# Gated mix of an S4D convolution and a bilinear GLU: one column's split tokens made twice instead of stored, and the last two rows summed from PSUM

## Chip, cores and metric

One core of one Trainium2 chip. The metric is the device time of one execution in microseconds (us), the median of three runs. Every operand and result is in f32. The engines are named as in the profile: PE (TensorE), DVE (VectorE), ACT (ScalarE), POOL (GpSimd), and SP, whose queue issues most of the DMA transfers.

## What is computed

```python
def _A_ref(u, ...):                       # S4D: a long convolution per channel
    dt = jnp.exp(log_dt)
    A = -jnp.exp(log_A_real) + 1j * A_imag
    C = (C_real + 1j * C_imag) * dt[:, None]
    P = jnp.exp((A * dt[:, None])[:, :, None] * pos[None, None, :])
    K = 2.0 * jnp.einsum("dn,dnl->dl", C, P).real
    Kf = jnp.fft.rfft(K, L2)              # L2 = 4096
    Uf = jnp.fft.rfft(u_t, L2)
    y = jnp.fft.irfft(Uf * Kf[None, :, :], L2)[:, :, :L]
    return y + u * D_skip
def _B_ref(x, w_gate, w_up, w_down):      # bilinear GLU
    h = (x @ w_gate) * (x @ w_up)
    return h @ w_down
x = A_u
g = sigmoid((x * gate_w).sum(-1, keepdims=True))
return g * _A_ref(x, ...) + (1 - g) * _B_ref(B_x, ...)
```

L = 2048 tokens, D = 512 channels, N = 128 states, F = 1792 hidden columns of the GLU.

## The kernel before, in words

**Who sets the order.** The kernel's functions don't issue instructions; they hand them to a planner (`Work.add`), each with an engine, an assumed duration, the tiles that it reads and writes, and a rank. `Work.run` then takes, over and over, the instruction that can start earliest by these assumed durations; among equals the lower rank goes first, then the one handed in first. `InOrder` issues them at one line, so all of them stand at L119 in the profile, and groups are told apart by the names of their tiles. A tile belongs to a tag with a fixed number of buffers, and tiles of a tag get their buffers strictly in the order in which they were created. A change in a few calls can therefore move instructions far away from it.

**The GLU.** The tokens are cut into four columns of 512 (`ci`), the hidden columns into 14 pieces of 128 (`f`), the pieces into four groups: f 0 to 2, 3 to 5, 6 to 9, 10 to 13 (L24). The loop of `glu` runs over groups and, in each, over the columns: 0, 1, 2, 3 in the first and third group (`gi` 0 and 2), 3, 2, 1, 0 in the second and fourth. A group so begins with the column that the one before it ended with, and its tokens are not loaded again there. Column 0 is used at the start, at the end of the second group and the start of the third, and as the last of all.

Products are made of three fp32r matmuls (low × high, high × low, high × high), so each operand is held split in a high and a low half. `tokens(gi, ci, kt)` brings one of the four tiles of a column (128 channels by 512 tokens). In the first group it loads 256 KB from `xT` into a buffer of the tag `raw`, ACT casts the high half into `xs`, DVE subtracts for the low half, and the split tile of 512 KB is stored in DRAM (`xs_d`). In later groups it loads these 512 KB back. The tag `xs` has 5 buffers, `raw` has 2; `raw` also carries the loads of the weights (`load`, L405; `split`, L411; `high`, L427; `rest`, L431).

`hidden(f)` makes the two products pg and pu for a piece and a column (24 matmuls of 512 columns: 2 products × 4 token tiles × 3), ACT copies pg to h, DVE multiplies h by pu, ACT casts hh and DVE subtracts hl. `down` multiplies these with the down weights (`dhi`, `dlo`) for four rows of 128 tokens, in PSUM tiles `y` (2 buffers). `evacuate` (L581) takes a finished y: ACT scales it by 1 − g into `acc`, and the row is stored to `out` (first group, by SP) or added to it by a DMA (later groups, by POOL). In the last group's last column the rows are kept instead, and `ends` (L599) loads what `out` holds so far into a tile `kt`, DVE adds the last parts of the convolution and then acc, and SP stores the row.

**The convolution** runs between the GLU's products on the same engines, in 16 blocks. DVE and ACT make tables `x` and `v` (one buffer for v), PE multiplies them (`k<-v,x`), and transforms of the kernel (`k<-kt,w1k_t`) and of u (`k<-in,w2s`) follow, a product on DVE, inverse transforms, and round trips through DRAM (`sk_d`, `su_d`, `y_d`).

Of the kernel before, what the change touches and what calls it, by code (L numbers as in the profile page):

```python
# [14 lines left out]
ALU = mybir.AluOpType  # L15
# [3 lines left out]
P = 128  # L19
L, D, N, F = 2048, 512, 128, 1792  # L20
KT = D // P
# [4 lines left out]
LAST = 3 if len(GROUPS) % 2 else 0  # L26
# [138 lines left out]
class Work:  # L165
# [27 lines left out]
    def add(self, engine, us, fn, r=(), w=(), rank=1, after=0.0, dma=0, hold=(), rows=(), many=0):  # L193


        task = Task(len(self.tasks), engine, us, fn, rank, after, dma)
        task.rows, task.many = rows, many
        self.tasks.append(task)
        clash = lambda p, q: p is None or q is None or p == q
        split = lambda x: x if isinstance(x, tuple) else (x, None)  # L200
        for tile, part in map(split, r):
            task.deps.update(t for p, t in tile.writers if clash(p, part))
        for tile, part in map(split, w):
            task.deps.update(t for p, t in tile.writers + tile.readers if clash(p, part))
        for tile, part in map(split, r):
            tile.readers.append((part, task))
        for tile, part in map(split, w):
            tile.writers.append((part, task))
        for tile, _ in map(split, [*r, *w, *hold]):
            if tile.pool and tile not in task.tiles:  # L210
                task.tiles.append(tile)
                tile.users.append(task)
        task.deps.discard(task)
        return task
# [105 lines left out]
def gated_mix_kernel(  # L320
# [16 lines left out]
    pe, dve, act, sp, pool_q = (InOrder(tc, e) for e in (nc.tensor, nc.vector, nc.scalar, nc.sync, nc.gpsimd))  # L337
    uv = u.rearrange("(p r) d -> p r d", r=NR)
    ov = out.rearrange("(p r) d -> p r d", r=NR)
    work = Work()  # L340
    add = work.add
# [12 lines left out]
    m_su, m_sk, m_y, m_out, m_xs, m_turn = (work.memory() for _ in range(6))  # L354
# [5 lines left out]
    def new(pool, tag, shape, dtype=F32, bufs=1, loose=False):  # L360
        return work.tile(pools[pool], tag, shape, dtype, bufs, loose)
# [14 lines left out]
    ngate = const.tile([P, NR], F32, name="ngate")  # L376
    m_gate = work.memory()
# [27 lines left out]
    def load(key, src, rank=0):  # L405
        if key in raws:
            return
        t = raws[key] = new("glu", "raw", [P, D], bufs=2)
        add("sp", 0.42, lambda: sp.dma_start(t.t, src), w=[t], dma=256, rank=rank)

    def split(hi, lo, s, key):  # L411

        t = raws[key]
        t, k = t if isinstance(t, tuple) else (t, None)
        src = lambda: t.t if k is None else t.t[:, k]
        got = t if k is None else (t, k)
        s, z = s if isinstance(s, tuple) else (s, s)
        ph, pl = (hi, s), (lo, z)
        at = lambda x, s: x.t if s is None else x.t[:, s] if hi is lo else x.t[:, s * D : (s + 1) * D]
        add("act", 0.62, lambda: act.copy(at(hi, s), src()), r=[got], w=[ph], rank=0)  # L420
        add(
            "dve", 0.69,
            lambda: dve.tensor_tensor(out=at(lo, z), in0=src(), in1=at(hi, s).bitcast(F32), op=ALU.subtract),
            r=[got, ph], w=[pl], rank=0,
        )
# [49 lines left out]
    def weights(fs):  # L475
        for f in fs:
            ws[f] = [new("glu", n, [P, 2 * D], F32R, SLOTS) for n in ("whi", "wlo")]
            if f == 0:
                for kt in range(KT):
                    first_split(kt)  # L480
                    if kt + 1 < KT:
                        tokens(0, 0, kt + 1)
                continue
            for c in range(2):
                load(("w", f, c), wts[f][:, c * D : (c + 1) * D])
                if f in GROUPS[0]:
                    split(*ws[f], c, ("w", f, c))
                else:
                    high(ws[f][0], c, ("w", f, c))
            if f not in GROUPS[0]:  # L490
                rest(*ws[f], wts[f][:, : 2 * D], 2)
# [23 lines left out]
    def tokens(gi, ci, kt):  # L515

        x = xs[kt] = new("glu", "xs", [P, 2, D], F32R, 5)
        if gi:
            add("sp", 0.42, lambda: sp.dma_start(x.t.bitcast(F32), xs_d[ci, kt]), r=[(m_xs, (ci, kt))], w=[x], dma=512, rank=0)
            return  # L520
        load(("x", gi, ci, kt), xT[kt * P : (kt + 1) * P, ci * D : (ci + 1) * D])
        split(x, x, (0, 1), ("x", gi, ci, kt))
        add("sp", 0.42, lambda: sp.dma_start(xs_d[ci, kt], x.t.bitcast(F32)), r=[x], w=[(m_xs, (ci, kt))], dma=512, rank=2)

    THREE = ((1, 0), (0, 1), (0, 0))
# [53 lines left out]
    ending = []  # L579

    def evacuate(gi, ci, r, y):  # L581
        t = 4 * ci + r
        final = gi == len(GROUPS) - 1 and ci == LAST
        acc = new("glu", "raw", [P, D], bufs=2) if final and r == 3 else new("glu", "acc", [P, D], bufs=3)
        add(
            "act", 0.69, lambda: act.activation(acc.t, y.t, AF.Copy, scale=ngate[:, t : t + 1]),
            r=[y, (m_gate, ci)], w=[acc], rank=0,
        )
        if final:
            ending.append((r, acc))  # L590
        elif gi == 0:
            add("sp", 0.42, lambda: sp.dma_start(ov[:, t, :], acc.t), r=[acc], w=[(m_out, t)], dma=256)
        else:
            add(
                "pool", 0.95, lambda: pool_q.dma_start(ov[:, t, :], acc.t, accum_op=ALU.add),
                r=[acc, (m_out, t)], dma=640, rows=[t],
            )

    def ends():  # L599

        t0 = 4 * LAST
        sums = new("tab", "kt", [P, 4, D])
        add(
            "sp", 0.42, lambda: sp.dma_start(sums.t, ov[:, t0 : t0 + 4, :]),
            r=[(m_y, (KT - 1, 0))], w=[sums, *((m_out, t0 + r) for r in range(4))], dma=1024, rows=range(t0, t0 + 4),
        )
        for r, acc in ending:
            t = t0 + r
            for q, (fin, parts) in late["fin"].items():
                add(  # L610
                    "dve", 0.25,
                    lambda r=r, q=q, t=t, fin=fin: dve.scalar_tensor_tensor(
                        sums.t[:, r, P * q : P * q + P], fin.t[:, 4 * (LAST % 2) + r], gate[:, t : t + 1],
                        sums.t[:, r, P * q : P * q + P], op0=ALU.mult, op1=ALU.add,
                    ),
                    r=[*parts, (m_gate, LAST)], w=[(sums, (r, q))], rank=0,
                )
            add(
                "dve", 0.69,
                lambda r=r, acc=acc: dve.tensor_tensor(  # L620
                    out=sums.t[:, r], in0=acc.t, in1=sums.t[:, r], op=ALU.add
                ),
                r=[acc], w=[(sums, (r, q)) for q in range(KT - 2, KT)], rank=0,
            )
            add(
                "sp", 0.42, lambda r=r, t=t: sp.dma_start(ov[:, t, :], sums.t[:, r]), r=[(sums, (r, q)) for q in range(KT - 2, KT)], w=[(m_out, t)],
                dma=256, rank=-1,
            )

    def glu():  # L630
        order = [(gi, ci) for gi in range(len(GROUPS)) for ci in (range(4) if gi % 2 == 0 else range(3, -1, -1))]
# [4 lines left out]
        for n, (gi, ci) in enumerate(order):  # L636
            fs = GROUPS[gi]
            if ci != old:
                for kt in range(KT):
                    tokens(gi, ci, kt)  # L640
            old = ci
            hs = {f: hidden(f) for f in fs}
            ends = n % 4 == 3 and gi + 1 < len(GROUPS)
            if ends:
                weights(GROUPS[gi + 1])

            for rr in ((0, 1), (2, 3)):
                ys = {r: new("ps_y", "y", [P, D], bufs=2) for r in rr}
                late = fs[-1:] if rr[0] == 0 else []
                for r in rr:  # L650
                    for f in fs:
                        if f not in late:
                            down(ys[r], r, hs[f], wd[f], f == fs[0], f == fs[-1])
                    if not late:
                        evacuate(gi, ci, r, ys[r])
                if late:
                    for r in rr:
                        down(ys[r], r, hs[fs[-1]], wd[fs[-1]], False, True)
                        evacuate(gi, ci, r, ys[r])
            if ends:  # L660
                down_weights(GROUPS[gi + 1])
# [701 lines left out]
    for b in range(NB):  # L1363
# [10 lines left out]
        if b % 4 == 3:  # L1374
            transforms(b // 4)
    ends()

    work.run()
# [53 lines left out]
```

## Time and profile before

| | us |
|---|---|
| runs | 601.52, 602.17, 602.39 |
| median | 602.17 |
| profiled execution, own time | 601.78 |
| its span in the trace | 600.0 |

| engine | busy us | share of the span |
|---|---|---|
| PE | 585.8 | 98% |
| DVE | 512.3 | 85% |
| ACT | 401.0 | 67% |
| POOL | 128.9 | 21% |

The times are those of whole executions; the trace begins a little later and ends a little earlier, so its span is 1.8 us shorter than the execution that it shows. Stretches are counted from the span's start. A wait is an engine's idle time ahead of an instruction, with the instruction that ended it; a landing is the time from a DMA's issue until its bytes are there.

### The profile page before, as it was taken

The page shows a single profiled execution, that of the slowest core. Times are in us where ns is not written, and L with a number is a line of the kernel's source. Part 1 is how long each engine was busy: PE and PEld are TensorE (multiplying, and loading weights), DVE is VectorE, ACT ScalarE, POOL GpSimd, SP SyncE. Part 2 cuts the span into 40 slices and gives each one's busy share as a digit, 9 for nine tenths or more (in the row PEclk, how much of TensorE's full clock was granted, in tenths as well). Part 3 has the DMA queues.
Part 4 walks back from the last instruction along what each step waited for, and adds up shares of the span by engine and source line. Part 5 has one row for each costly group of instructions (what it writes and reads, how often), then busy time and mean ns, then how long its engine had stood idle before and what let it go on. Part 6 is the DMA issues. An engine that isn't in the chain of part 4 may idle for free.

```text
span 600.0 us, 15878 instructions
## 1 busy us (share of the span) xinstructions
PE 585.8 (98%) x6500; PEld 443.4 (74%) x6500; DVE 512.3 (85%) x811; ACT 401.0 (67%) x893; POOL 128.9 (21%) x191
## 2 busy tenths in 40 slices
PE   8899999999999999999999999999999999999996
PEld 5657777777877787887777877866878777767674
DVE  6999999999998997999999999978999933486525
ACT  5279787999678479967959764979984423433522
POOL 0011212221204131310133301104353023201111
PEclk9989999999999999999999999999999999999998
DMA  8899979699869699996959945999999569959976
GB/s 276 314 357 340 336 281 338 187 207 253 232 175 227 166 241 248 195 229 163 302 135 266 215 129 171 226 250 239 182 203 260 95 159 355 244 153 264 279 141 122
DMA packets 71867, 137.33 MB, mean 229 GB/s; under 512 B 7156, under 2 KB 35828, under 8 KB 69364
## 3 DMA queue, kind: packets, MB, share of 16 engines
q1 hardware_dynamic: 47476, 88.21, 45.9%
q0 software_dynamic: 23904, 47.98, 40.4%
q8 instruction: 51, 0.84, 0.6%
q10 hardware_dynamic: 416, 0.13, 0.1%
q14 instruction: 20, 0.16, 0.1%
HBM read 81.25 MB, written 55.05 MB: 227 GB/s over the span
## 4 chain that ended last, share of the span: by engine, by line
PE 79%; DVE 8%; ACT 6%; DMA 5%; issue 1%; ACTq 0%; DVEq 0%
PE y L119 22%; PE pu L119 21%; PE pg L119 21%; PE k L119 15%; DMA raw<-in_wts 4%; DVE x L119 2%; DVE y L119 1%; DVE v L119 1%; ACT ts L119 1%; ACT whi L119 1%; DMA y<-in_xT 1%; ACT L119 1%; DVE h L119 1%; DVE t L119 1%; DVE xs L119 1%
## 5 line engine op out<-in xcount | busy, mean ns | idle before, releaser
L119 PE MATMUL pg<-xs,whi 128*128 128x512 f32 x448 | 139.2, 392 | 1.0 <-DVE xs L119 0.7
L119 PE MATMUL pu<-xs,whi 128*128 128x512 f32 x448 | 138.7, 391 | 0.0
L119 PEld LDWEIGHTS pg<-xs,whi 128*128 128x128 f32 x448 | 84.5, 189 | 20.0 <-ACT whi L119 2.0
L119 PEld LDWEIGHTS pu<-xs,whi 128*128 128x128 f32 x448 | 84.4, 188 | 17.1
L119 PE MATMUL y<-dhi,hl 128*128 128x512 f32 x224 | 90.5, 404 | 2.2 <-DVE x L119 1.1
L119 PE MATMUL pu<-xs,wlo 128*128 128x512 f32 x224 | 90.1, 402 | 0.9 <-issue 0.5
L119 PE MATMUL pg<-xs,wlo 128*128 128x512 f32 x224 | 90.1, 402 | 0.8 <-ACT whi L119 0.5
L119 PE MATMUL y<-dlo,hh 128*128 128x512 f32 x224 | 87.5, 391 | 1.3 <-DVE dlo L119 1.3
L119 PE MATMUL y<-dhi,hh 128*128 128x512 f32 x224 | 87.4, 390 | 0.0
L119 POOL DMA_DIRECT2D out<-acc x44 | 38.4, 954 | 184.8 <-ACT acc L119 173.8
L119 ACT COPY ev<-k 128x512 f32<-128x512 f32 x112 | 59.2, 595 | 15.7 <-PE k L119 15.6
L119 ACT CAST hh<-h 128x512 fp32r<-128x512 f32 x56 | 34.7, 620 | 43.3 <-DVE h L119 43.2
L119 ACT ACTIVATE acc<-y,ngate 128x512 f32<-128x512 f32 x63 | 42.8, 686 | 30.6 <-PE y L119 28.2
L119 DVE TENSOR_TENSOR h<-pu,h 128x512 f32<-128x512 f32 x56 | 38.6, 689 | 23.0 <-PE pu L119 22.2
L119 PEld LDWEIGHTS y<-dhi,hl 128*128 128x128 f32 x224 | 42.0, 188 | 21.7 <-issue 6.2
L119 PEld LDWEIGHTS pu<-xs,wlo 128*128 128x128 f32 x224 | 42.1, 188 | 19.2 <-issue 9.8
L119 PEld LDWEIGHTS pg<-xs,wlo 128*128 128x128 f32 x224 | 42.0, 188 | 19.1 <-issue 6.8
L119 ACT COPY h<-pg 128x512 f32<-128x512 f32 x56 | 33.1, 590 | 29.7 <-PE pg L119 27.8
L119 PEld LDWEIGHTS y<-dlo,hh 128*128 128x128 f32 x224 | 42.1, 188 | 9.5 <-DVE dlo L119 1.7
L119 PEld LDWEIGHTS y<-dhi,hh 128*128 128x128 f32 x224 | 42.1, 188 | 9.1
L119 DVE TENSOR_TENSOR hl<-h,hh 128x512 fp32r<-128x512 f32 x56 | 38.5, 687 | 8.4 <-ACT hh L119 8.4
L119 POOL DMA_DIRECT2D su_d<-ev x32 | 17.3, 549 | 90.2 <-ACT ev L119 90.2
(127 smaller groups left out, 1015.7 us busy)
## 6 DMA issues: line engine op xcount, KB each, us to landing
xs<-xs_d SPq DMA_DIRECT2D x36, 512.0 KB, 7.8
out<-acc POOLq DMA_DIRECT2D x44, 256.0 KB, 7.1
raw<-in_wts SPq DMA_DIRECT2D x36, 256.0 KB, 5.2
xs_d<-xs SPq DMA_DIRECT2D x16, 512.0 KB, 7.1
su_d<-ev POOLq DMA_DIRECT2D x32, 256.0 KB, 5.3
y_d<-ts SPq DMA_DIRECT2D x14, 512.0 KB, 6.5
in<-su_d POOLq DMA_DIRECT2D x24, 256.0 KB, 8.4
sk_d<-ev SPq DMA_DIRECT2D x6, 1024.0 KB, 6.2
```

What stands on the lines that cost most here:

```text
L119: got = getattr(self.engine, name)(*args, **kw)
```

## The change

**Tokens.** In the first group the tiles of column 0 are split but no longer stored. At the end of the second group, where column 0 comes again, its tiles are loaded from `xT` and split again, and stored then; the fourth group reads them back as before.

**End.** In the last column of the last group, rows 2 and 3 aren't copied by ACT any more. DVE sums them with a multiply-add that reads y from PSUM and scales it by 1 − g. The last row is summed and stored in two halves of 256 columns, the second half by ACT's queue. Rows 0 and 1 are still copied, and DVE adds them with the same kind of instruction and scale 1.

```diff
     def tokens(gi, ci, kt):
...
-        if gi:
+        if gi > (ci == 0):
             add("sp", 0.42, lambda: sp.dma_start(x.t.bitcast(F32), xs_d[ci, kt]), r=[(m_xs, (ci, kt))], w=[x], dma=512, rank=0)
             return
         load(("x", gi, ci, kt), xT[kt * P : (kt + 1) * P, ci * D : (ci + 1) * D])
         split(x, x, (0, 1), ("x", gi, ci, kt))
+        if gi == 0 == ci:
+            return
         add("sp", 0.42, lambda: sp.dma_start(xs_d[ci, kt], x.t.bitcast(F32)), r=[x], w=[(m_xs, (ci, kt))], dma=512, rank=2)
...
     def evacuate(gi, ci, r, y):
...
-        acc = new("glu", "raw", [P, D], bufs=2) if final and r == 3 else new("glu", "acc", [P, D], bufs=3)
+        if final and r > 1:
+            ending.append((r, y))
+            return
+        acc = new("glu", "acc", [P, D], bufs=3)
...
-                    r=[*parts, (m_gate, LAST)], w=[(sums, (r, q))], rank=0,
+                    r=[*parts, (m_gate, LAST)], w=[(sums, (r, 1))], rank=0,
                 )
-            add(
-                "dve", 0.69,
-                lambda r=r, acc=acc: dve.tensor_tensor(
-                    out=sums.t[:, r], in0=acc.t, in1=sums.t[:, r], op=ALU.add
-                ),
-                r=[acc], w=[(sums, (r, q)) for q in range(KT - 2, KT)], rank=0,
-            )
-            add(
-                "sp", 0.42, lambda r=r, t=t: sp.dma_start(ov[:, t, :], sums.t[:, r]), r=[(sums, (r, q)) for q in range(KT - 2, KT)], w=[(m_out, t)],
-                dma=256, rank=-1,
-            )
+            for n, cs in enumerate((slice(0, D // 2), slice(D // 2, D)) if r == 3 else (slice(0, D),)):
+                part = [(sums, (r, k)) for k in (range(2) if r < 3 else (n,))]
+
+                def total(r=r, t=t, acc=acc, cs=cs):
+                    scale = 1.0 if r < 2 else ngate[:, t : t + 1]
+                    dve.scalar_tensor_tensor(
+                        sums.t[:, r, cs], acc.t[:, cs], scale, sums.t[:, r, cs], op0=ALU.mult, op1=ALU.add
+                    )
+
+                add("dve", 0.42 if r == 3 else 0.69, total, r=[acc, (m_gate, LAST)], w=part, rank=0)
+                e, q = ("act", act) if n else ("sp", sp)
+                add(
+                    e, 0.42, lambda r=r, t=t, cs=cs, q=q: q.dma_start(ov[:, t, cs], sums.t[:, r, cs]), r=part,
+                    dma=128 if r == 3 else 256, rank=-1,
+                )
```

The planner's order changes in many places. Three of them, each first as it was and then as it is now. The numbers in the names tell tiles apart and differ from one order to the other.

The first is SP's queue at the start of the program, from the last of the first loads on; `xs_d` is the DRAM copy of the split tokens, `in<-in_u` the first load of u, `raw<-in_wts` the down weights of f=2 and `raw<-in_xT` the first tokens of column 1. Before:

```order
L119 DMA v_142<-in_prm 128x1024
L119 DMA xs_d_60<-xs_135 128x1024
L119 DMA xs_d_60<-xs_148 128x1024
L119 DMA xs_d_60<-xs_168 128x1024
L119 DMA xs_d_60<-xs_184 128x1024
L119 DMA in_206<-in_u 128x2048
L119 DMA dt_d_91<-small_90 128x4
L119 DMA raw_273<-in_wts 128x512
L119 DMA raw_283<-in_xT 128x512
```

Now:

```order
L119 DMA v_142<-in_prm 128x1024
L119 DMA in_202<-in_u 128x2048
L119 DMA dt_d_91<-small_90 128x4
L119 DMA raw_269<-in_wts 128x512
L119 DMA raw_279<-in_xT 128x512
```

The four stores are gone from here, and the loads behind them have moved up.

The second is SP's queue in the second group. Before, the first weights of the third group (f=6 and f=7, in `raw`) are loaded among the tokens of the second group's columns:

```order
L119 DMA raw_1630<-in_wts 128x512
L119 DMA raw_1689<-in_wts 128x512
L119 DMA xs_1706<-xs_d_60 128x1024
L119 DMA xs_1776<-xs_d_60 128x1024
L119 DMA raw_1788<-in_wts 128x512
L119 DMA xs_1799<-xs_d_60 128x1024
L119 DMA xs_1811<-xs_d_60 128x1024
L119 DMA raw_1817<-in_wts 128x512
```

Now the raws of column 0's tokens have the two buffers at that place, and the first weights of the third group come behind the last of these, with the stores between them:

```order
L119 DMA raw_2140<-in_xT 128x512
L119 DMA xs_d_60<-xs_2125 128x1024
L119 DMA sk_d_58<-ev_2138 128x2048
L119 DMA sk_d_58<-ev_2211 128x2048
L119 DMA w2s_2457<-in_w2 128x256
L119 DMA raw_2502<-in_xT 128x512
L119 DMA xs_d_60<-xs_2481 128x1024
L119 DMA raw_2511<-in_wts 128x512
L119 DMA xs_d_60<-xs_2488 128x1024
L119 DMA w2s_2564<-in_w2 128x256
L119 DMA xs_2574<-xs_d_60 128x1024
L119 DMA raw_2595<-in_wts 128x512
```

The weights have moved behind the tokens, toward the end of the second group.

The third is PE behind the last hidden product of the third group's first column (`pu`); `y` are down products, whose `dhi`, `dlo` are down weights of one f each, `pg` is the next column's first product, and `whi`, `wlo` are its weights. Before, the rows from there are these, and 41 more down products and two groups of the convolution follow before a new token tile is read, apart from the one (`xs_2516`) loaded early into the fifth buffer:

```order
L119 MATMUL pu_3576<-xs_2509,whi_3059 128x512 x2
L119 MATMUL y_3614<-dhi_3128,hl_3359 128x512
L119 MATMUL y_3614<-dlo_3210,hh_3285 128x512
L119 MATMUL y_3614<-dhi_3128,hh_3285 128x512
L119 MATMUL y_3614<-dhi_3215,hl_3425 128x512
L119 MATMUL y_3614<-dlo_3218,hh_3417 128x512
L119 MATMUL y_3614<-dhi_3215,hh_3417 128x512
L119 MATMUL y_3614<-dhi_3279,hl_3555 128x512
```

Now the down products of one f for two rows stand there, and then the next column's products begin with the tile in the fifth buffer (`xs_2574`):

```order
L119 MATMUL pu_3572<-xs_2572,whi_3206 128x512 x2
L119 MATMUL y_3612<-dhi_3390,hl_3344 128x512
L119 MATMUL y_3612<-dlo_3401,hh_3340 128x512
L119 MATMUL y_3612<-dhi_3390,hh_3340 128x512
L119 MATMUL y_3626<-dhi_3390,hl_3344 128x512
L119 MATMUL y_3626<-dlo_3401,hh_3340 128x512
L119 MATMUL y_3626<-dhi_3390,hh_3340 128x512
L119 MATMUL pg_3632<-xs_2574,wlo_2824 128x512
L119 MATMUL pg_3632<-xs_2574,whi_2602 128x512 x2
L119 MATMUL pu_3641<-xs_2574,wlo_2824 128x512
```

Six more down products and one group of the convolution (`k<-kt,w1k_t`) follow, and then products with the tiles loaded next (`xs_3591`, `xs_3605`, `xs_3609`). The down products of the other pieces have moved behind these.

## The prediction

> **What bounds the kernel now.** I read the page first: busy time by engine, then the chain that ended last.
>
> ```profile
> PE 585.8 (98%) x6500; PEld 443.4 (74%) x6500; DVE 512.3 (85%) x811; ACT 401.0 (67%) x893; POOL 128.9 (21%) x191
> ...
> PE 79%; DVE 8%; ACT 6%; DMA 5%; issue 1%; ACTq 0%; DVEq 0%
> ```
>
> TensorE is the bound: 98% of the span and 79% of the chain. VectorE comes next with 85%. The table by stretch says how close it is, and where (columns: us, then busy time and count of PE, PEld, DVE, ACT and POOL, granted clock, DMA share, GB/s).
>
> ```profile
> 15.00:480.00 465.00, 459.71 (x5035) 351.48 (x5034) 443.37 (x685) 350.67 (x795) 105.41 (x140) 1.00 0.87 231
> 480.00:594.00 114.00, 113.12 (x1428) 83.75 (x1426) 58.31 (x95) 40.77 (x82) 22.51 (x26) 1.00 0.86 215
> ```
>
> Between 15 and 480 us PE is idle 5.3 us, DVE 21.6 us. After 480 us DVE is busy about half the time and PE is idle 0.9 us in 114. So there are three places in which the change can act: the start, where PE does wait; the tables that DVE makes for the convolution, which must stay ahead of PE; and the few us behind PE's last matmul. Everything else is PE's own work, and the change adds and removes none: the order of before and that of the change have 2803 rows each on PE.
>
> **Part 1: the stores leave the start.** The SP timeline of 9.5 to 18.5 us (start, us, queue, transfer) shows what stands there.
>
> ```profile
> 9.79 3.76 SPq L119 DMA_DIRECT2D xs_d<-xs  x4
> 13.98 0.51 SPq L119 DMA_DIRECT2D in<-in_u  x1
> 16.27 0.32 SPq L119 DMA_DIRECT2D dt_d<-small  x1
> 16.77 0.58 SPq L119 DMA_DIRECT2D raw<-in_wts  x1
> 18.02 0.33 SPq L119 DMA_DIRECT2D raw<-in_xT  x1
> ```
>
> From issue to landing, the four stores took (first row) and the two raw loads (second):
>
> ```profile
> DMA to landing us min/median/max: 9.4/9.6/10.0
> DMA to landing us min/median/max: 9.0/9.3/9.6
> ```
>
> Four stores of 512 KB hold SP from 9.79 to 13.55, and their bytes are on the way until about 23 (13.55 + 9.6). The u load and the two raw loads are issued behind them. Without them SP comes to the u load about 4 us sooner, and 2 MB fewer are ahead of the raws (down weights of f=2, tokens of column 1). What those late landings cost: the first raw's cast on ACT, three rows of the table of PE's waits (us in total, times, longest), the stretch by windows, and one group of the convolution in it.
>
> ```profile
> 26.40 0.62 ACT L119 CAST dhi<-raw 128x512 fp32r<-128x512 f32 x1 [1.24 <-DMA raw<-in_wts]
> ```
>
> ```profile
> PE y L119 <- DVE dlo L119: 1.3, 1, 1.3
> PE y L119 <- DVE x L119: 1.1, 1, 1.1
> PE y L119 <- ACT acc L119: 0.9, 2, 0.6
> ```
>
> ```profile
> 27.00:29.00 2.00, 0.59 (x2) 0.27 (x2) 2.00 (x7) 0.64 (x2) 0.00 (x0) 1.00 0.69 157
> 30.00:34.00 4.00, 3.45 (x10) 2.24 (x9) 3.95 (x10) 2.42 (x10) 0.00 (x0) 0.57 0.99 395
> 25.86:46.16 20.30, 16.65 (x80) 10.07 (x80) 20.25 (x40) 12.95 (x41) 2.35 (x4) 0.92 0.89 318
> ```
>
> ```profile
> 42.93 1.11 PE L119 MATMUL k<-in,w2s 32*64 32x512 f32 x16
> ```
>
> The cast of dhi waits for its raw until 26.40; its matmuls, and those of dlo behind it, are the waits of 1.1 (the row names x, but that matmul reads dhi) and 1.3 us. PE works 0.59 of the 2 us from 27 to 29, and from 30 to 34 the granted clock is 0.57, which takes (1 − 0.57) × 4 = 1.7 us from it. From 25.86 to 46.16, 20.3 us pass with 80 PE records: 32 are two groups of the convolution like the last row, 1.1 us each, and 48 are GLU matmuls, which start 0.226 us apart where nothing disturbs them (the first two rows of part 4 are 14 matmuls apart: 593.95 − 590.78 = 3.17). That is 48 × 0.226 + 2 × 1.1 = 13.1 us of work. So **7.2 us** is lost here, and that bounds the gain: 0 to −7.2. I walked the new order through with these durations. About 2.7 us of waits stay: the first product of column 1 now stands ahead of the last down products and waits for its tokens (about 1.0), the accumulator copies still come late (0.9), and so does u's first group (0.8). I assume no half-clock stretch. I take 7.2 − 2.7 = **−4.5 us**.
>
> [...]
>
> **Part 2: what the tables give back.** The convolution makes 16 blocks of a kernel table; each starts with matmuls k<-v,x that need DVE's tables. For one block the last DVE row of a table and the matmuls that read it; the wait of PE for such a table over the whole run; and the rows of a token split.
>
> ```profile
> 117.05 0.65 DVE L119 TENSOR_TENSOR v<-v,sq 128x256 f32<-128x256 f32 x1
> ...
> 117.82 2.07 PE L119 MATMUL k<-v,x 128*32 128x64 f32 x128
> ```
>
> ```profile
> PE k L119 <- DVE v L119: 0.3, 1, 0.3
> ```
>
> ```profile
> L119 DVE TENSOR_TENSOR xs<-raw,xs 128x512 fp32r<-128x512 f32 x12 | 8.1, 685 | 0.2 <-ACT xs L119 0.2
> L119 ACT CAST xs<-raw 128x512 fp32r<-128x512 f32 x12 | 7.3, 620 | 1.2 <-DMA raw<-in_xT 0.6 <-PE pu L119 0.5
> ```
>
> PE starts 0.12 us after this table is done (117.05 + 0.65), and once it waits 0.3 us for one: the two run neck and neck, and PE hardly pays yet. A PE that is 4.5 us ahead meets tables that are not: DVE is idle only 21.6 us over 465, and its work isn't spread to suit. It also gets four more subtractions, 4 × 0.685 = 2.7 us, and ACT four more casts, 4 × 0.620 = 2.5 us (hidden beside PE, since ACT has 114 us free in the same stretch; without that cover at most 2.5). Some of DVE's idle time at the start goes with the waits there. Bounds: nothing is given back (0) or the whole lead and the 2.7 us besides (+7.2). The nearest row, 117.05, has no slack at all, so I take most of the lead: **+3.0**, and −1.5 stays.
>
> **Part 3: the tokens of column 0 in the second group.** Four loads of 512 KB become four of 256 KB through the two raw buffers, which also carry the weights of the third group. In the order SP now brings the weights of f=6 behind the last two of these raws. The third group's down weights so come later, and the down products of its first column are cut into small pieces: at the first change of column, the work that stands between the release of the first old token tile and the first product with a new one shrinks from 61 matmuls and two groups of the convolution to 28 matmuls and one group (40 and one to the third new tile). The landings of the old loads there, two rows at the start of the old cover, and one such group:
>
> ```profile
> DMA to landing us min/median/max: 10.4/13.9/16.9
> ```
>
> ```profile
> 277.48 0.39 PE L119 MATMUL y<-dhi,hl 128*128 128x512 f32 x1
> 277.70 0.39 PE L119 MATMUL y<-dlo,hh 128*128 128x512 f32 x1
> ...
> 291.29 2.00 PE L119 MATMUL k<-kt,w1k_t 32*128 32x512 f32 x16
> ```
>
> The old cover was 61 × 0.226 + 2 × 2.0 = 17.8 us, just over the slowest landing, and no wait for xs shows there. New cover: 28 × 0.226 + 2.0 = 8.3 us to the first tile, 40 × 0.226 + 2.0 = 11.0 us to the third; the loads land after 10.4 to 16.9 us, median 13.9. Median against the longer cover, 13.9 − 11.0 = 2.9 us; the slowest against the shorter, 16.9 − 8.3 = 8.6. Fewer bytes beside them could bring them under the cover: 0. I take **+4.0 us**, nearer the median. Should this wait drop the clock, as the one at 27 us did, it would cost the same 1.7; I leave that in the range. [...] Behind a waiting product stand all of PE's later rows, and the h copies and products of ACT and DVE wait for them, so this wait is paid in full.
>
> The four stores themselves are read only in the last column of the fourth group. But on SP they stand among the raws: each waits for its DVE subtraction, and the loads behind it wait with it. I price that inside the +4.0, as it too makes the third group's weights late.
>
> **Part 4: the end.** A down product some us before the end and the last rows of before, the issue of the last store, the landings of the last four stores, and the nearest row for a sum from PSUM over 256 columns:
>
> ```profile
> 590.78 0.39 PE L119 MATMUL y<-dhi,hl 128*128 128x512 f32 x1
> ...
> 593.95 0.39 PE L119 MATMUL y<-dhi,hh 128*128 128x512 f32 x1
> 594.38 0.69 ACT L119 ACTIVATE raw<-y,ngate 128x512 f32<-128x512 f32 x1 [2.03 <-PE y L119]
> 595.10 0.69 DVE L119 TENSOR_TENSOR kt<-raw,kt 128x512 f32<-128x512 f32 x1 [2.02 <-ACT raw L119]
> ```
>
> ```profile
> 595.82 0.33 SPq L119 DMA_DIRECT2D out<-kt  x1
> ```
>
> ```profile
> DMA to landing us min/median/max: 2.8/4.9/6.1
> ```
>
> ```profile
> L119 DVE TENSOR_TENSOR kt<-k,kt 128x256 f32<-128x256 f32 x32 | 13.4, 419 | 4.5 <-ACT kt L119 4.4
> ```
>
> Before: ACT 0.69, DVE 0.69 and two handovers of 0.03 from 594.38 to 595.82. After: no ACT, DVE reads PSUM in two halves. A 256-column sum from PSUM takes 419 ns; two of them, one after the other, 0.84 us, so the second store starts at 594.38 + 0.84 + 0.03, against 595.82: −0.57. Its piece has half the bytes, worth perhaps 0.1 of the 2.8 us landing: **−0.64**, bounds −0.3 (a multiply-add from PSUM dearer than this sum, or ACT's queue slower) to −1.0. If instead the table's last sum isn't loaded in time, the gain goes; but before, all four sums waited for ACT, and none for the table's load.
>
> **Sum.** 601.78 us is the profiled execution's own time (span 600.0). −4.5 + 3.0 + 4.0 − 0.64 = +1.9, so 603.7 for that execution. It lies 0.39 below the median shown, 602.17; against the median, **604.1 us**.
>
> **Rivals.**
>
> *A, faster: the lead is kept and the cover suffices.* Place: PE's change of column in the third group (290 us before), and DVE's idle 21.6 us. If the loads land within 8.3 to 11.0 us there, and DVE, which waits for PE in part of its idle time, moves forward with it, only −4.5 − 0.64 stays: 602.17 − 5.1 = 597.0 us. For it: raws landed in 9.0 to 9.6 at the start; against it: 10.4 as the fastest of the four loads in question, and a table with 0.12 us of slack.
>
> *B, slower: the tables are the bound.* All the lead is given back and the 2.7 us of subtractions come on top, since they stand ahead of tables that PE waits for; with the third group's wait +2.7 + 4.0 − 0.64 = +6.1 − up to 1.5 that overlaps: 606.7 to 608.2. For it: 0.12 us at 117 us. Against it: DVE has idle time, and ACT's and DVE's new work has 20 us to be done in.
>
> *C, no change: the stores only move.* The u load and raws land as late as before, because other loads fill the gap (DMA share is 0.87 over the 465 us), and the third group's loads just fit: 602.17 − 0.64 = 601.5.
>
> **Chances.** A measurement of this kernel tells about 0.2% (1.2 us) from no change: faster is under 600.97, slower over 603.37. Forecast (604.1, itself 602.2 to 607) 0.44, of which 0.04 lies within 0.2%; A 0.26 (0.25 faster, 0.01 same); B 0.12, slower; C 0.18 (0.14 same, 0.04 faster). Faster 0.29, same 0.19, slower 0.52. Range: it takes in the forecast, B and C whole, and the upper part of A. Under 598.5 I leave out 0.14 (from A with all of the 7.2 us, 594, to just over A's centre), over 608.5 about 0.06 (a wait of 8.6 and a halved clock): 598.5 to 608.5.
>
> **What would show it.** Part 1: the first raws cast at about 21 us instead of 26.40, no stretch at half clock near 31 us, and the group of 42.93 some 4 us earlier. Part 2: PE idle before k<-v,x at more blocks than the one of before, put down to DVE v. Part 3: a wait of PE at pg<-xs or pu<-xs of 3 to 5 us between 280 and 300 us, put down to the DMA of xs. Part 4: 0.9 us from PE's last matmul to the last store's issue, not 1.5. I am wrong if PE's wait in the third group is under 1 us, or if DVE's tables move forward as much as PE does.

## The result, and the profile after

The changed kernel takes **616.8 us** (median of 4, 614.84 to 627.1) against 601.85 (median of 4, 601.17 to 602.39): 1.0238 times the time before, 95% interval 1.0206 to 1.027. The forecast of 604.1 had the sign right, and its range (598.5 to 608.5) misses the time by 8 us. The ratios leave out slow executions, those over 1.5% above the fastest of the same kernel or at a far lower granted clock; of the changed kernel's that is the one of 627.1 us.

The page of the changed kernel, in the same parts as in the prediction, with PE's and the clock's rows of the 40 slices:

```profile
span 615.8 us, 15892 instructions
...
PE 590.5 (96%) x6500; PEld 444.6 (72%) x6500; DVE 514.9 (84%) x816; ACT 401.4 (65%) x895; POOL 128.7 (21%) x191
...
PE   8999999999999999997999599999999999999997
...
PEclk9999999999999999999999699999999999999999
...
PE 50%; DVE 17%; DMA 16%; issue 7%; ACT 7%; POOL 1%; SPq 1%; DVEq 0%; POOLq 0%; ACTq 0%
```

PE has as many matmuls as before, 6500, and 4.7 us more busy time; its mean granted clock in this execution is 0.988 instead of 0.994. It holds 50% of the chain instead of 79%, and DMA 16% instead of 5%. Two slices are new: the 19th (277 to 293 us) and the 23rd (339 to 354), the second with a lower clock. The table of PE's waits names what stands in them (us in total, times, longest):

```profile
PE k L119 <- DMA in<-sk_d: 6.5, 1, 6.5
PE pg L119 <- ACT h L119: 3.5, 4, 1.3
PE pg L119 <- DMA xs<-xs_d: 2.7, 1, 2.7
PE k L119 <- DVE kt L119: 1.7, 1, 1.7
```

To see where time goes, I count PE's work by its matmuls, each at the mean step of its kind in the trace before, and compare when the same amount was done in the two traces. Negative is ahead of before, in us:

| time in the trace before | 42 | 64 | 94 | 157 | 279 | 289 | 331 | 341 | 486 | 590 |
|---|---|---|---|---|---|---|---|---|---|---|
| changed kernel | −3.4 | −3.6 | −2.2 | −0.2 | +0.6 | +7.0 | +6.8 | +16.3 | +16.0 | +17.5 |

So there is a lead of 3.6 us, of which 0.2 is left at 157; a loss of 6.4 between 279 and 289; a loss of 9.5 between 331 and 341; 1.8 more in the other stretches from 157 on; and an end that is 1.7 shorter, since the spans differ by only 15.8. Each place in the trace:

**The third group's change of column.** PE's timeline:

```profile
283.98 2.08 PE L119 MATMUL k<-kt,w1k_t 32*128 32x512 f32 x16 [1.68 <-DVE kt L119]
...
290.31 0.50 PE L119 MATMUL pg<-xs,wlo 128*128 128x512 f32 x1 [2.66 <-DMA xs<-xs_d]
```

and the stretch behind it (the clock is the third number from the right):

```profile
290.00:294.00 4.00, 3.69 (x13) 2.42 (x13) 4.00 (x7) 2.88 (x6) 0.00 (x0) 0.61 1.13 391
```

The reader is to see two waits, 1.68 and 2.66 us, and a price behind them: the clock at 0.61 for 4 us costs (1 − 0.61) × 4 = 1.6 us more.

**POOL's queue at 317 to 346 us**, and PE there:

```profile
321.07 1.55 POOL L119 DMA_DIRECT2D out<-ts  x1 [2.48 <-ACT kt L119]
328.92 1.57 POOL L119 DMA_DIRECT2D out<-ts  x1 [6.30 <-issue]
329.83 2.09 POOL L119 DMA_DIRECT2D in<-su_d  x2
331.25 1.35 POOL L119 DMA_DIRECT2D in<-sk_d  x1
342.44 0.69 POOL L119 DMA_DIRECT2D in<-sk_d  x1 [9.84 <-issue]
```

```profile
339.25 0.39 PE L119 MATMUL y<-dhi,hh 128*128 128x512 f32 x1
346.12 1.06 PE L119 MATMUL k<-in,w2s 32*32 32x256 f32 x4 [6.48 <-DMA in<-sk_d]
```

```profile
342.00:354.00 12.00, 7.79 (x78) 4.87 (x79) 2.88 (x5) 3.78 (x7) 6.09 (x8) 0.57 0.95 190
```

Two accumulations of 512 KB (`out<-ts`) stand back to back in POOL's order, with the loads that PE needs behind them. The second is issued only at 328.92. Three loads follow it at once, the fourth 9.84 us later: "issue" means that no semaphore of the profile held POOL. How long the two accumulations took from issue to landing, and, for the third load alone (331.25), who waited for it and its landing:

```profile
DMA to landing us min/median/max: 7.5/10.4/13.2
...
  PE k L119: 6.5, 1
...
DMA to landing us min/median/max: 14.6/14.6/14.6
```

The second accumulation lands 13.2 us behind its issue, at 342.1, and the third load 14.6 us behind its own, at 345.9. PE's wait of 6.48 us ends with that landing. So PE waits for a load that was issued 8 us before PE came to it (339.64) but landed behind the accumulation; the fourth load, issued late, lands 1.3 us after it, and PE needs it next. The clock then stays down, 0.57 over the 12 us and 0.50 from 346 to 352: about 3 us more, and 6.5 + 3.0 is the loss of 9.5.

**The end**: PE's last matmul, DVE's two halves, the last store, and the landings of the last five stores:

```profile
611.44 0.39 PE L119 MATMUL y<-dhi,hh 128*128 128x512 f32 x1
611.87 0.88 DVE L119 SCALAR_TENSOR_TENSOR kt<-y,ngate,kt 128x256 f32<-128x256 f32 x2 [1.97 <-PE y L119]
...
612.78 0.35 ACTq L119 DMA_DIRECT2D out<-kt  x1
```

```profile
DMA to landing us min/median/max: 1.7/2.0/2.9
```

From the end of PE's last matmul to the last issue it is 0.95 us (before: 1.48), and to the end of the span 3.97 (before: 5.66). The stores land in 1.7 to 2.9 us where they took 2.8 to 6.1.

### The profile page after: what moved, and what is told of

The parts are those of the page before. It is cut to its first block, busy times and chain, and to the rows that moved or that the text cites. A ratio compares the mean times of both kernels' runs of the same rounds, so it can differ in the third digit from the quotient of the medians.

```text
span 615.8 us, 15892 instructions
## 1 busy us (share of the span) xinstructions
PE 590.5 (96%) x6500; PEld 444.6 (72%) x6500; DVE 514.9 (84%) x816; ACT 401.4 (65%) x895; POOL 128.7 (21%) x191
## 4 chain that ended last, share of the span: by engine, by line
PE 50%; DVE 17%; DMA 16%; issue 7%; ACT 7%; POOL 1%; SPq 1%; DVEq 0%; POOLq 0%; ACTq 0%
PE pg L119 14%; PE pu L119 13%; PE y L119 13%; PE k L119 10%; DMA raw<-in_wts 5%; DVE x L119 3%; DVE v L119 3%; DMA in<-sk_d 2%; DVE y L119 2%; DMA xs<-xs_d 2%; DMA ev<-in_wts 2%; DMA par_d<-v 2%; DMA dlo<-in_wts 1%; DVE hl L119 1%; DVE h L119 1%
## 5 line engine op out<-in xcount | busy, mean ns | idle before, releaser
L119 PEld LDWEIGHTS y<-dlo,hh 128*128 128x128 f32 x224 | 42.4, 189 | 10.4 <-issue 2.5
L119 PE MATMUL k<-in,w2s 32*32 32x256 f32 (+1 forms) x896 | 29.5, 435 | 6.6 <-DMA in<-sk_d 6.5
```

Source lines behind the costliest of these rows:

```text
L119: got = getattr(self.engine, name)(*args, **kw)
```

## The experiments

My theory after reading this: the loss is not in the change's own instructions but in the new order, in which single waits stand that the planner doesn't count. The rival: the change's transfers and second splits cost it, in any order. Three kinds of kernel tell them apart: one part of the change in the order of before; the changed kernel with one thing moved; and the kernel before in other orders.

**The end alone** (`e1_tail`): the diff's edits of `evacuate` and `ends` on the kernel before. PE's order is the same.

> The kernel before with the change's end alone (rows 2 and 3 summed from PSUM by DVE, the last in halves); the order of everything ahead of the last rows is that of before. By the prediction's part 4 the end gains 0.64 us, 601.5 against 602.17. By what the trace of the changed kernel shows (3.97 us from the end of PE's last matmul to the end of the span, against 5.66 before) it gains about 1.7 us: 600.2 to 600.5. If the shorter end in that trace came from other transfers being done by then and not from the edit, the gain is 0.5 (one handover and ACT's copy less) or under.

Measured: 602.32 us, ratio 1.000 (0.9976 to 1.0025); an interval of 1.5 us to either side can't tell 0.64 from nothing. Its trace can: the last store is issued 0.95 us behind PE's last matmul, as in the changed kernel, but the end of the span comes 5.7 us behind it, as before. So the third of these holds, and nothing is gained in the trace. Two kernels tell why.

**The way cleared** (`e14_tail_clear`, `e15_old_clear`): the new end and the old one, both without the last two accumulations, and executed once each.

```diff
+                (lambda: None) if q == KT - 1 else
                 lambda rs=rs, flat=flat: pool_q.dma_start(ov[:, rs[0] : rs[-1] + 1, cs], flat(), accum_op=ALU.add),
```

> The kernel before with the change's end alone, and the last two accumulations of POOL (out<-x, 512 KB and 256 KB) left out, so that the last quarter of the channels lacks the convolution's part in some rows. Theory 1 (the end of the kernel before is set by these two transfers, which the last stores have to share the way with): from the end of PE's last matmul to the end of the span 5.7 us with them becomes 4.0 to 4.3 us without, as in the changed kernel. Theory 2 (the end is that of the last store alone): 5.4 to 5.8 us, as with them.

> The kernel before with its own end and the same two accumulations left out. Theory 1: 4.5 to 4.9 us from the end of PE's last matmul to the end of the span, so that the edit of the end is worth 0.5 to 0.6 where the way is clear, and nothing where it isn't. Theory 2: 5.6 us, as in the kernel before.

The two ends, new and old, each the last matmul and the last store's issue:

```profile
594.76 0.39 PE L119 MATMUL y<-dhi,hh 128*128 128x512 f32 x1
...
596.10 0.35 ACTq L119 DMA_DIRECT2D out<-kt  x1
```

```profile
593.01 0.39 PE L119 MATMUL y<-dhi,hh 128*128 128x512 f32 x1
...
594.88 0.33 SPq L119 DMA_DIRECT2D out<-kt  x1
```

The spans are 599.1 and 598.2 us, so from PE's end (595.15 and 593.40) 4.0 and 4.8 us remain, against 5.7 and 5.66 with the accumulations. Theory 1 holds, with a larger difference than its 0.5 to 0.6: the new end is worth about 0.85 us where the way is clear (0.53 at the last issue, and the last stores land in 1.7 to 2.1 us instead of 2.0 to 2.1) and nothing where two accumulations are still on it. In the changed kernel the order had brought them forward: the later of them was issued 8 us ahead of PE's end (603.83 to 611.83), before the change 4.3 (589.99 to 594.34).

**The stores alone** (`e3_nostore`): the order of before, column 0's stores not issued, and its later loads sent to column 1's tiles.

```diff
-        add("sp", 0.42, lambda: sp.dma_start(xs_d[ci, kt], x.t.bitcast(F32)), r=[x], w=[(m_xs, (ci, kt))], dma=512, rank=2)
+        store = (lambda: None) if ci == 0 else lambda: sp.dma_start(xs_d[ci, kt], x.t.bitcast(F32))
+        add("sp", 0.42, store, r=[x], w=[(m_xs, (ci, kt))], dma=512, rank=2)
```

> The kernel before in its own order, with the four stores of column 0's split tokens in the first group left out and nothing in their place; column 0's later loads read column 1's tiles, so the output's rows of column 0 are computed from other tokens. It measures the start of the change by itself, without the second splitting and without a new order. Theory 1 (the lead is given back at DVE's tables, whatever the rest of the order): PE is 3 to 4.5 us ahead at 50 us and under 1 us ahead by 150 us, and the time falls by under 1 us, to about 601.5. Theory 2 (the lead was lost in the changed kernel to its new order and its new splits only): PE keeps 3 us or more to the end, and the time is 597.5 to 599.

Measured: 602.25 us, ratio 0.9987 (0.9968 to 1.0006). Neither theory holds: there is no lead to give back, 0.3 us at 64 us and 0.3 at the end. The rows of ACT and DVE around the load that I had blamed, with this load's cast on ACT and its subtraction on DVE:

```profile
24.91 0.62 ACT L119 CAST dhi<-raw 128x512 fp32r<-128x512 f32 x1
...
26.19 0.69 DVE L119 SCALAR_TENSOR_TENSOR x<-x 128x512 f32<-128x512 f32 x1
...
28.01 0.69 DVE L119 TENSOR_TENSOR dlo<-raw,dhi 128x512 fp32r<-128x512 f32 x1
...
28.75 0.50 PE L119 MATMUL y<-dlo,hh 128*128 128x512 f32 x1 [1.86 <-DVE dlo L119]
```

The cast no longer waits: 24.91 instead of 26.40. But DVE is full (busy for all 2 us from 27 to 29), and its order puts a table (26.19) and two scores ahead of the subtraction, which starts at 28.01 (before: 28.18). PE waits 1.86 us for it instead of 1.34, and 0.56 for the matmul ahead of it instead of 1.05: 2.42 us in all, where it was 2.39. In the changed kernel the same subtraction stands at another place of DVE's order:

```profile
25.04 0.68 DVE L119 TENSOR_TENSOR dlo<-raw,dhi 128x512 fp32r<-128x512 f32 x1
```

**One DVE instruction moved** (`e11_dlo`): the same kernel, with that subtraction put ahead of the table and the two scores in DVE's order (and its cast handed out before it).

> The kernel before without the four stores of column 0 (as in the run without them, with column 1's tiles read for column 0 later), and with one DVE instruction moved: the subtraction dlo<-raw,dhi of f=2 goes ahead of three table and score operations, from 28.0 to about 26.2 us. Theory 1 (PE's early waits are those of DVE's fixed order, and the earlier landing is of use only where DVE's order takes it up): PE's wait of 1.86 us for dlo falls under 0.3, and PE is 1.5 to 3.5 us ahead of the kernel before at 50 us. Theory 2 (the early loss is due to other things, such as the late scale of the copies): PE gains under 0.7 us at 50 us. In both, what is left of a lead at 150 us tells whether the tables take it back.

Measured: 601.99 us, ratio 0.9997 (0.9988 to 1.0007). The wait for dlo is gone, as theory 1 said, but its lead of 1.5 to 3.5 us isn't there: 0.2 us at 50 and at 64 us, which is what theory 2 said. The next wait for DVE takes its place, and the clock falls later, from 34 us on:

```profile
26.26 0.69 DVE L119 TENSOR_TENSOR dlo<-raw,dhi 128x512 fp32r<-128x512 f32 x1
...
30.04 0.74 PE L119 MATMUL pg<-xs,whi 128*128 128x512 f32 x2 [1.40 <-DVE xs L119]
```

```profile
34.00:38.00 4.00, 4.00 (x14) 3.16 (x13) 4.00 (x6) 2.49 (x12) 0.00 (x0) 0.66 0.87 345
```

So the lead needs more of the changed order than this one row. Which rows of it suffice was not tried.

**POOL's second accumulation moved** (`e4_poolmove`): the changed kernel in its own order, but for one entry of POOL's queue (from the built orders; `-` is the changed kernel).

```diff
 L119 DMA out_0<-ts_3937 128x8x128
+L119 DMA in_4196<-su_d_57 64x8x128 x2
+L119 DMA in_4196<-sk_d_58 64x8x128 x2
 L119 DMA out_0<-ts_3930 128x8x128
-L119 DMA in_4197<-su_d_57 64x8x128 x2
-L119 DMA in_4197<-sk_d_58 64x8x128 x2
```

> The changed kernel in its own order but for one POOL instruction: the second 512 KB accumulation out<-ts, issued at 328.92 us in its trace, is moved behind the four loads in<-su_d, in<-su_d, in<-sk_d, in<-sk_d that stand behind it. Theory 1 (that accumulation fills POOL's queue and the loads for k<-in,w2s stand behind it): PE's wait of 6.5 us for in<-sk_d near 340 us and the half-clock stretch behind it go, and the time falls by 7 to 10 us, to 607 to 610. Theory 2 (the transfers as a whole are the limit there, with four token loads of 512 KB at the same time): the wait only shrinks by a few us or moves to another load, and the time falls by under 4 us.

Measured: 607.69 us, ratio 1.0088 (1.0057 to 1.0119): 9 us less than the changed kernel. PE is +5.7 at 331 us and +5.5 at 341, where the changed kernel loses 9.5. Theory 1 holds: PE's wait hung on that accumulation, though the load that PE needed was not kept from being issued but landed behind it. The same stretch before the change, in the changed kernel and with the entry moved:

```profile
330.00:350.00 20.00, 20.00 (x383) 15.89 (x382) 18.96 (x27) 14.59 (x29) 6.26 (x8) 1.00 1.12 241
330.00:350.00 20.00, 13.43 (x165) 8.74 (x164) 14.72 (x21) 8.42 (x14) 7.85 (x11) 0.80 1.05 238
330.00:350.00 20.00, 20.00 (x321) 15.24 (x320) 19.85 (x31) 14.97 (x26) 6.84 (x8) 1.00 1.11 243
```

With the entry moved PE is busy for all 20 us again, at full clock, with the DMA engines no less loaded than in the changed kernel (1.11 against 1.05). The four token loads of 512 KB are still there, so they are not the cause.

**Weights ahead of tokens** (`e6_weights_first`): f=6's weights handed to the planner before column 0's second tokens.

```diff
+                if (gi, ci) == (1, 0):
+                    weights(GROUPS[2][:1])
                 for kt in range(KT):
                     tokens(gi, ci, kt)
...
-                weights(GROUPS[gi + 1])
+                weights(GROUPS[gi + 1][gi == 1 :])
```

> The changed kernel, with the first piece of the third group's weights (f=6) handed to the planner ahead of column 0's second tokens, so that these weights get the two raw buffers first. In the new order 24 down products stand again between the last product with the old tokens and the next column's, as before the change. Theory 1 (the third group's stall of 6.4 us came from the token loads taking the raw buffers ahead of the weights): no wait of PE for xs or kt between 275 and 300 us, PE there is within 1.5 us of the kernel before, and what the order does to POOL's queue near 340 us decides the rest: 600 to 608. Theory 2 (the stall is due to the extra split work or to the transfers around it): 3 us or more are still lost between 275 and 300 us.

Its executions took 602.24, 612.34, 613.87 and 614.86 us; the trace is of the first. In it theory 1 holds: PE is level with before from 279 to 300 us, and no wait stands there.

```profile
275.00:300.00 25.00, 25.00 (x243) 18.41 (x242) 24.38 (x36) 22.31 (x56) 3.41 (x4) 1.00 0.98 267
```

This execution has all the transfers and splits of the change and takes as long as the kernel before, so they need not cost anything by themselves. Why the other three took 10 us more is open: none of them was profiled.

**Both** (`e9_both`): the same, with POOL's second accumulation behind the four loads.

> The kernel with f=6's weights ahead of the second tokens, and the second out<-ts of POOL moved behind the four loads that follow it, as in the earlier run with this move. That kernel without the move took 602.24 us in its profiled execution and 612.3 to 614.9 in three others. Theory 1 (its long executions meet the same POOL wait as the changed kernel, and the profiled one just escapes it): 599 to 604 in all executions. Theory 2 (their cause lies elsewhere): still 610 or more in some executions.

Measured: 615.03 us, ratio 1.0222 (1.0162 to 1.0281): theory 2. In this trace PE's time goes elsewhere. It waits 2.56 us for ACT's h at 138 us (the lead falls from 3.3 to 0.2, with the clock at 0.57 over the 4 us from 138), 5.46 us at 221 within one group of tables, and 3.7 us for ACT's h near 270.

```profile
213.81 2.04 PE L119 MATMUL k<-v,x 128*32 128x64 f32 x126
221.31 0.42 PE L119 MATMUL k<-v,x 128*32 128x64 f32 x2 [5.46 <-issue]
```

In the profiled execution of the kernel without the move, the two waits for h are 1.74 and 2.47 us, the clock stays up behind both (1.00), and the stop within the tables isn't there.

**Other orders of the same work** (`e7_before_step`, `e8_after_step`, `e12_rate31`, `e12_rate29`): one constant of the planner changed, T_STEP from 9.85 to 9.80 or the assumed transfer rate DMA_RATE from 0.30 to 0.31 or 0.29.

> The kernel before with one number of the planner changed, T_STEP from 9.85 to 9.80: the same instructions and transfers in another order. Theory 1 (much of the changed kernel's loss is that of a new order as such, which meets waits that the planner doesn't count): 604 to 615. Theory 2 (the loss is due to the change's own transfers and splits, and a new order without them costs nothing): 600.5 to 603.5.

> The changed kernel with T_STEP 9.80 in place of 9.85: the same work as in the changed kernel, in another order. Theory 1 (the wait of 6.5 us for in<-sk_d and the stall of the third group belong to one order): the time moves by more than 3 us, up or down, and PE's wait for in<-sk_d near 340 us is not there or of another size. Theory 2 (they belong to the change): 613 to 620 with the same two waits.

> The kernel before with the planner's assumed transfer rate 0.31 in place of 0.30: the same instructions and transfers, in another order. Theory 1 (most of the changed kernel's loss is what any new order of this kernel costs, since its waits are not in the plan): 605 to 620. Theory 2 (the loss needs the change's second splits and moved loads): 600.5 to 604.

> The same the other way: the assumed rate 0.29, a second order of the kernel before. Theory 1: 605 to 620, at other waits than with 0.31. Theory 2: 600.5 to 604.

The first came out in exactly the order of before, so it is no test; it repeats the kernel before, at 1.0007 (0.9996 to 1.0018). The second, 621.99 us, is 1.0336 (1.0278 to 1.0395) of the kernel before: theory 1, since it is 5 us slower than the changed kernel and the wait of 6.5 us isn't in it. Most of its loss stands elsewhere, 11.6 us of it past 486. The other two are the kernel before in new orders, with nothing of the change: **616.25 us**, 1.0204 (1.0134 to 1.0273), and **609.01 us**, 1.0096 (1.0068 to 1.0124). The first waits of PE in these two:

```profile
PE y L119 <- ACT acc L119: 5.0, 2, 3.4
PE y L119 <- issue: 4.1, 2, 2.7
PE k L119 <- issue: 3.2, 2, 1.7
PE pg L119 <- ACT h L119: 2.8, 1, 2.8
```

```profile
PE pg L119 <- ACT xs L119: 3.7, 1, 3.7
PE y L119 <- DVE dlo L119: 2.5, 1, 2.5
```

Where PE stands against the kernel before, by the same count as above (us):

| time in the trace before | 64 | 157 | 279 | 289 | 331 | 341 | 486 | 590 |
|---|---|---|---|---|---|---|---|---|
| stores alone | −0.3 | −0.5 | −0.5 | −0.5 | −0.7 | −0.7 | −0.6 | −0.3 |
| POOL moved | −4.1 | −1.0 | −0.6 | +5.9 | +5.7 | +5.5 | +5.5 | +5.7 |
| weights first | −5.3 | −2.8 | 0.0 | 0.0 | +0.6 | +0.5 | +1.8 | +1.7 |
| both | −4.9 | 0.0 | +13.9 | +14.0 | +14.8 | +14.7 | +16.3 | +15.8 |
| changed, step 9.80 | −3.8 | +1.5 | +8.2 | +10.9 | +10.4 | +11.7 | +13.6 | +25.2 |
| before, rate 0.31 | −1.4 | +2.4 | +6.0 | +6.2 | +5.8 | +5.5 | +12.3 | +14.8 |
| before, rate 0.29 | +7.0 | +7.0 | +7.1 | +7.1 | +6.3 | +6.6 | +7.2 | +7.2 |

Theory 1 holds for these two: both orders of the unchanged work lose, 1 and 2%, each at other places. No kernel here beats the kernel before beyond its interval.

## Why the prediction was wrong, point by point

- **What bounds it: right.** PE is the bound and PE's work is unchanged; what moved is PE's waiting and the clock behind it.
- **Part 1, a lead of 4.5 us because the stores leave the start: the size was near by luck, the reason wrong.** The lead is 3.6 us at 64 us, and the clock stays up from 30 to 34 us (1.00), as assumed. But without the stores and with nothing else changed it is 0.3. The step that failed is the reading of the wait as the load's: the cast of dhi did wait for its load, but without that wait PE only waits longer at the next matmul (2.42 us for the two instead of 2.39). It waits there for DVE, which was full and took the subtraction in its turn. The row said so ("DVE dlo"). Why the changed order keeps its lead is not shown.
- **Part 2, +3.0 given back: the size near by luck, the mechanism wrong.** 3.4 us are given back by 157 us, but k<-v,x waits only 0.4 us for v in the whole run, and no table is late. By the count above three places make up 3.2 of it: 0.9 at a down product at 88, where DVE is late with hl; 1.05 at 138, where PE waits 1.33 us for ACT's h (0.28 before); and 1.25 at a down product at 151, where POOL's load of low weights is late.

```profile
88.09 0.50 PE L119 MATMUL y<-dhi,hl 128*128 128x512 f32 x1 [0.82 <-DVE hl L119]
```

```profile
151.57 0.47 PE L119 MATMUL y<-dlo,hh 128*128 128x512 f32 x1 [1.12 <-DMA dlo<-in_wts]
```

- **Part 3, +4.0 at the third group: the place and cause right, the size short.** It is 6.4, of which three terms make up 5.9: 2.66 for the tokens, against the 2.9 of the prediction's median landing; 1.68 for a table transform's kt, which I hadn't looked at; and 1.6 of clock, which I had left in the range. In the profiled execution with the weights first it is gone.
- **Part 4, −0.64 at the end: it is −1.7 in the changed kernel, 0 by itself, −0.85 with the way clear.** The working of the handovers was right to 0.1 us (1.48 to 0.95 at the issue). What failed is that the end was taken to follow the last issue: in the trace of the end alone the last stores, with the accumulations ahead of them, land in 3.4 to 5.9 us, without them in 1.7 to 2.1. The halves also took 0.48 us each, not 0.419.
- **What wasn't in the sum: 9.5 us at 341.** This term puts the time out of the range. I read the order at the three places where the diff acts, and costed all else as unchanged. POOL's order had changed in the middle of the convolution: two accumulations side by side, where before a load stood between. The step that failed is "Everything else is PE's own work": here PE waited 6.48 us for a load that landed behind the second accumulation, and lost 3 us more of clock. With that one entry of POOL's order moved, the time is 607.69 us, inside the range. Of the rivals none was of this kind; B (606.7 to 608.2) had the right side for a reason that isn't there.

What DVE pays for an operand in PSUM can be read in two pairs here. In the changed kernel the multiply-add over 512 columns takes 749 ns from PSUM and 692 from SBUF, 0.057 us more. Before the change the plain product h<-pu,h from PSUM takes 689 and the plain sum kt<-acc,kt from SBUF 686, only 0.003 us more.

## What to carry to other kernels

Where a planner or list scheduler writes the order, an edit's price is not that of its instructions. Compare the whole order on every engine, not the places where the diff acts, and look for new neighbours in each queue: two long transfers side by side, with a load that PE needs behind them. And make the null test: another order of the same work. Here two of them cost 1 and 2%; two are too few to say that any new order would lose, but enough that the price of an edit of this size can't be told from that of its order unless the order is held fixed.

## What the runs showed of the hardware

- POOL stopped issuing with no semaphore of the profile in the way, and went on when a transfer of its own had landed. Behind a 512 KB accumulation (the second out<-ts, 328.92) three more DMAs were issued, and the fourth 9.84 us later, 0.3 us after that accumulation had landed (342.14); the second accumulation itself had waited 6.30 us behind the first and was issued 0.35 us after that one's landing. In the traces of before, of the changed kernel, of POOL moved and of weights first, all 12 such stops of over 1 us end 0.26 to 0.39 us behind a landing of one of POOL's transfers. How much can be on the way before POOL stops, no run here shows.
- The clock fell behind a wait of 2.56 us and stayed up behind one of 2.47. Two waits for ACT's h, in the runs with the weights first (the first row and its stretch) and with both edits (the second):

```profile
261.96 0.50 PE L119 MATMUL pg<-xs,wlo 128*128 128x512 f32 x1 [2.47 <-ACT h L119]
```

```profile
260.00:264.00 4.00, 2.04 (x9) 1.71 (x10) 3.72 (x5) 4.00 (x8) 0.57 (x1) 1.00 0.86 179
```

```profile
138.17 0.80 PE L119 MATMUL pg<-xs,wlo 128*128 128x512 f32 x1 [2.56 <-ACT h L119]
```

```profile
138.00:142.00 4.00, 3.83 (x10) 3.07 (x11) 3.85 (x7) 4.00 (x9) 0.03 (x1) 0.57 0.87 169
```

  Behind 2.47 us it stays at 1.00, and in the next 4 us too; behind 2.56 it is 0.57 over 4 us, 1.7 us lost. What decides between the two outcomes, at waits 0.09 us apart, no run here shows.
- PE stopped for 5.46 us in the middle of a group of 128 equal matmuls (both edits, 221.31) with no semaphore of the profile in the way ("issue"). Such stops of over 1 us stand in three of the other orders, at several kinds of matmul (1.36 to 5.46 us), and not in the kernel before or the changed one, where they stay under 0.7. In the traces of the eleven kernels whose PE was followed here, each of the 20 such stops of over 0.4 us ends 1.2 to 1.7 us behind the end of a transfer of the instruction queue, though there are only 51 of these in some 600 us. The one in the stop of 5.46 us (in the stretch from 215.8 to 221.4 us) runs from 218.58 to 219.91, and PE goes on at 221.31:

```profile
q8 instruction: 1, 0.02, 1.5%
```

  So these stops and these transfers go together; whether PE stops because of them is not shown, since no run here moves them.
